# Four interleaved layers on one core: which head group VectorE takes, 163 adding transfers, epsilon on GpSimd

## The chip, the cores and the metric

One core of a Trainium2 chip runs the whole program in one launch. TensorE (PE) multiplies, VectorE (DVE), ScalarE (ACT) and GpSimd (POOL) work on tiles of 128 partitions, and SyncE (SP) and GpSimd start the DMA transfers. PSUM has eight banks of 128 x 512 float32 values here. The metric is the device time of one execution in microseconds (us), lower is better. The time of the kernel before is the median of three executions.

## The reference

The input x has 2048 rows of 512 values. Four layers are added to it in turn: A, B, A, B, with the same weights for both A and both B.

```python
def _A_ref(x, wq, wk, wv, wo):          # 32 query heads of 16, one key and value head
    q = (x @ wq).reshape(B, S, H, Dh).transpose(0, 2, 1, 3)
    k = x @ wk
    v = x @ wv
    scores = einsum("bhqd,bkd->bhqk", q, k) * (Dh ** -0.5)
    p = softmax(scores, axis=-1)
    o = einsum("bhqk,bkd->bhqd", p, v)
    return o.transpose(0, 2, 1, 3).reshape(B, S, H * Dh) @ wo
def _B_ref(x, wqkv, wo):                # linear attention, 32 heads of 16
    pq, pk = phi(q), phi(k)             # phi(t) = where(t > 0, t + 1, exp(t)) + 1e-6
    kv = einsum("bhsd,bhse->bhde", pk, v)
    z = einsum("bhsd->bhd", pk)
    o = einsum("bhqd,bhde->bhqe", pq, kv) / (einsum("bhqd,bhd->bhq", pq, z) + 1e-6)
    return o.transpose(0, 2, 1, 3).reshape(B, S, D) @ wo
x = x + A(layernorm(x)); x = x + B(layernorm(x)); x = x + A(layernorm(x)); x = x + B(layernorm(x))
```

The layer norm adds 1e-5 (epsilon) to the variance and has no weights.

## The kernel before

**The plan.** The kernel has no fixed loops over instructions. A planner (class Planner) runs a small simulation while the program is being built: every operation has an assumed duration, an assumed latency after it, a priority and the operations it depends on. When an engine of the simulation is free, the ready operation of the lowest priority number is put next on that engine. The order that comes out is written into the program; on the chip each engine follows its own order and waits on semaphores. A wrong duration in the plan doesn't make a wrong result, it makes an engine wait behind an operation whose input isn't there yet. Transfers have a cost of their own in the plan: a queue time `dmaq` is pushed forward by the first number of `xfer`, and the transfer lands the second number after that.

**Layer A (run_a, L = 0 and 2).** Queries are cut into 16 tiles of 128 rows, keys into 16 tiles of 128, and the 32 heads into two halves (par) of four groups j = 0..3 with four heads each. A block is one key tile with one head group: a score matmul writes 128 keys x (4 heads x 128 queries) into one PSUM bank (line 958). There are 64 blocks for each query tile and half, 2048 a layer. They are held in segments (class Seg): `left` lists the blocks not yet taken, `need[j]` counts the value matmuls that group j will take. Four value matmuls, one for each group, run side by side on TensorE, each in 32 of its columns (line 1012); a segment is done when each group has had its `need[j]`, and a round that lacks a group leaves that quarter of the array idle.

**Two ways to the exponential.** ScalarE takes groups of two or three blocks in one instruction (line 1134, function act_stream) and leaves bfloat16 probabilities in a PT buffer. VectorE takes single blocks (functions alone, dve_open, dve_split, dve_take): one add and maximum writes an int16 whose bits, read as bfloat16, are a rough exponential (line 1215). To make it exact enough, three shifted copies of it are needed, so that four value matmuls with four weighted copies of V stand for one. A block on VectorE thus raises `need[j]` by three. The copies are made for four blocks (a chunk, 128 x 2048) at a time: an add of a constant on VectorE (line 1263, dve_shifts), or, for at most one of the three copies of a chunk, an **adding transfer** (line 1292, dma_shift). For that, SyncE first fills a free FB buffer with the constant (the filling transfer, line 1283, prime) from a row `shift_row` (cst) in device memory, and GpSimd then starts a DMA that adds the chunk onto it. FB buffers are the working store of VectorE's way: 12 of their own, and others lent from tiles that rest (xn, wq, wo2, sacc, OBB), which is why the profile shows the same step under several tile names.

**Who takes which block.** ScalarE's groups never hold the same head group twice; Seg.take(js) gives the first block of the group with the most blocks left that isn't in js. VectorE takes from the back of a segment some way ahead of ScalarE (dve_pick: over `CHT` blocks ahead, `ENDL` at the end), by the same rule. VectorE starts when all keys of the layer are there (KGATE).

**Numbers that steer it.** BLO, BLS, BLT and DXB bound VectorE's backlog at which it is given another block; FBO, FBS and FBP are counts of free FB buffers kept back; DQ bounds the backlog of `dmaq` at which an adding transfer is still taken; PGEN, DPF, DXF and DTAIL are the plan's times of a transfer (starting it, filling, adding, landing); DMIN stops the transfers before the last segments. TUNE[0] is set at layer 0 and stays; TUNE[2] is put over it at layer 2.

**Layer norm (ln_tile, line 801).** For each of 16 tiles and four layers: statistics on VectorE (lines 810, 811), variance plus epsilon into ve on VectorE (line 812), the power -0.5 into rs on GpSimd (line 814), then the normalised tile xn on VectorE (line 817), which is transposed for the projections.

**Layer B (run_b)** lies mostly beside the attention of its neighbours.

**The start.** GpSimd fills FB buffer 11 with the constant (line 691) and SyncE writes one row of it to device memory as shift_row (line 692), with low priority, among the constants of the start.

Of the kernel before, what the change touches and what calls it, by code (L numbers as in the profile page):

```python
# [7 lines left out]
FP32 = mybir.dt.float32  # L8
I16 = mybir.dt.int16
ACTF = mybir.ActivationFunctionType  # L10
ALU = mybir.AluOpType

PE, AC, DV, PO, SP = "pe", "act", "dve", "pool", "sp"
ENGS = (PE, AC, DV, PO, SP)

P = 128
S, D, H, DH = 2048, 512, 32, 16
T = S // P
# [325 lines left out]
class Seg:  # L344
# [11 lines left out]
    def take(self, js, back=False):  # L356
        n = [sum(1 for b in self.left if b[1] == j) for j in range(4)]
        js = [j for j in range(4) if j not in js and n[j]]
        if not js:
            return None if back else self.left.pop(0)  # L360
        j = max(js, key=lambda j: n[j])
        mine = [b for b in self.left if b[1] == j]
        b = mine[-1] if back else mine[0]
        self.left.remove(b)
        return b
# [13 lines left out]
LAG = 0.15  # L379
# [16 lines left out]
BLS = 1.4  # L396
BLO = 5.0
DXB = 2.0
BLT = 2.5
# [11 lines left out]
ENDL = 12  # L411
NSH = 4
# [6 lines left out]
FBO = 2  # L419
FBS = 4  # L420
AHEAD = 20
CHT = 19
PSH = False
STICK = 1.5
# [3 lines left out]
DSH = 1  # L428
DMIN = 4
NPRE = 2  # L430
PGEN = 1.1
DPF = 2.5
DXF = 4.5
DTAIL = 2.5
DQ = 4.0
FBP = 6
TUNE = {0: {"FBS": 5, "AHEAD": 15, "LAG": 0.15, "ENDL": 12, "FBO": 0, "BLO": 7.0, "DXB": 1.6, "BLT": 3.2},
        2: {"FBS": 3, "DXB": 1.6, "ENDL": 9, "BLS": 1.0}}


def bass_interleave_layers__grouped_kv_mqa__linear_attn_block__prompt_kernel(
# [12 lines left out]
    op = pl.op  # L454
    sb = nc.alloc_sbuf_tensor
# [18 lines left out]
    xn = sb("xn", [P, NXN, D], BF16)  # L474
    st = sb("st", [P, T, 2, 6], FP32)
    mv = sb("mv", [P, T, 2], FP32)
    ve = sb("ve", [P, T], FP32)
    rs = sb("rs", [P, T], FP32)
    mhalf = sb("mhalf", [P, 1], FP32)
    ident = sb("ident", [P, P], BF16)  # L480
    mask8 = sb("mask8", [P, 8, 17], BF16)
# [11 lines left out]
    NFB = 12  # L493
    FB = sb("FB", [P, NFB, CHB * 512], BF16)
# [179 lines left out]
    def pool_op(fn, writes, reads=(), dur=0.2, prio=0.0):  # L674
        return op({PO: (dur, fn)}, reads=reads, writes=writes, prio=prio)
# [10 lines left out]
    cst = nc.dram_tensor("shift_row", (1, CHB * 512), I16, kind="Internal").ap()  # L686

    def fb_keys(i):
        return [("FB", i, h) for h in range(CHB)]

    pool_op(lambda e: e.memset(FB[:, NFB - 1, :].bitcast(I16), DSH * 128 // NSH), fb_keys(NFB - 1), dur=1.2, prio=8.0)
    op({SP: (0.54, lambda e: e.dma_start(cst, FB[0:1, NFB - 1, :].bitcast(I16)))}, reads=fb_keys(NFB - 1), writes=["cst"], prio=8.0, lat=2.5, dma=True)
    pool_op(lambda e: e.memset(kmask[:, 1:2], KSC), ["kmask"], dur=0.1)
    for j in range(4):
        for r, v in ((0, KSC), (1, 0.0)):
# [42 lines left out]
    def until(*keys):  # L738
        for k in keys:
            yield ("ops", pl.ws(k))  # L740
# [60 lines left out]
    def ln_tile(L, t, prio, far=False, crit=False):  # L801
        c = ring(L, t)
        hk = host(L, ("xnT", c)) if c >= 4 else ()
        cols = slice(c * P, (c + 1) * P)
        if t in two:
            two.discard(t)
            n = 2
        else:
            n = 1
            op({DV: (0.6, lambda e: e.bn_stats(st[:, t, 0, :], x_sb[:, t, :]))}, reads=[("x", t)], writes=[("st", t)], prio=prio, lat=0.13)  # L810
        op({DV: (0.09, lambda e: e.bn_aggr(mv[:, t, :], st[:, t, 0:n, :]))}, reads=[("st", t)], writes=[("mv", t)], prio=prio, lat=0.13)
        op({DV: (0.07, lambda e: e.tensor_scalar(out=ve[:, t:t + 1], in0=mv[:, t, 1:2], scalar1=1e-5, scalar2=None, op0=ALU.add))},  # L812
           reads=[("mv", t)], writes=[("ve", t)], prio=prio, lat=0.16)
        op({PO: (0.55, lambda e: e.tensor_tensor(out=rs[:, t:t + 1], in0=ve[:, t:t + 1], in1=mhalf[:], op=ALU.pow))},  # L814
           reads=[("ve", t), "mhalf"], writes=[("rs", t)], prio=prio - 9.0)
        i = yield ("acq", xn_pool, prio)
        op({DV: (0.325, lambda e: e.tensor_scalar(out=xn[:, i, :], in0=x_sb[:, t, :], scalar1=mv[:, t, 0:1], scalar2=rs[:, t:t + 1],
                                                op0=ALU.subtract, op1=ALU.mult))},
           reads=[("x", t), ("mv", t), ("rs", t)], writes=[("xn", i)], prio=prio, port=True, behind=host(L, ("xn", i)) if i >= 2 else ())
        if far:  # L820
            o = dmat(xnT[:, :, cols], xn[:, i, :], [("xn", i)], [("xnT", c)], prio, hk)
            pl.give_after(xn_pool, i, [o])
            return
        yield from until(("xn", i))
        if crit:
            bs = yield from acq2(prio)
            o = tr2(xn[:, i, :], [("xn", i)], bs, prio)
            pl.give_after(xn_pool, i, [o])
            halves(bs, lambda h: xnT[:, 2 * h:2 * h + 2, cols], ("xnT", c), prio, lambda b, h: bank_bf(b)[:, 0:2, :], hk)
            return  # L830
        b = yield ("acq", banks, prio)
# [117 lines left out]
    def run_a(L):  # L949
# [114 lines left out]
        def act_stream():  # L1064
# [11 lines left out]
            while True:  # L1076
# [3 lines left out]
                while len(group) < size[s_] and split is None and state["si"] < len(segs):  # L1080
                    sg = segs[state["si"]]
                    if not sg.left:
                        state["si"] += 1
                        if state["si"] == len(segs) - BACK:
                            recall([("FB", NFB + 4), ("FB", NFB + 5)])
                        continue
                    if len(group) == GA - 1 and size[s_] == GA:
                        split = dve_split({g_[2] for g_ in group})
                        if split is not None:
                            continue  # L1090
                    js = {g_[2] for g_ in group}
                    blk = sg.take(js)
                    while any(("K", L, kt) not in pl.flags for kt in (sg.kts if L else blk[:1])) or ("Q", L, sg.t) not in pl.flags:
                        if group:
                            break
                        yield ("flag", next((("K", L, kt) for kt in (sg.kts if L else blk[:1]) if ("K", L, kt) not in pl.flags), ("Q", L, sg.t)))
                    else:
                        group.append((sg,) + blk)
                        continue
                    sg.left.insert(0, blk)  # L1100
                    break
# [4 lines left out]
                n = len(group)  # L1106
# [64 lines left out]
        def dve_pick(js):  # L1171
            si = state["si"]
            ahead = 0
            for k in range(si, si + 5):
                if k >= len(segs):
                    continue
                sg = segs[k]
                ahead += len(sg.left)
                if ahead <= (CHT if si < len(segs) - 1 else ENDL):
                    continue  # L1180
                if len(sg.left) > sg.blocks * (1.0 - DMAX) and all(("K", L, kt) in pl.flags for kt in sg.kts) and ("Q", L, sg.t) in pl.flags:
                    b_ = sg.take(js | {x[2] for x in chunk["blk"] if x[0] is sg}, back=True) or sg.take(js, back=True)
                    if b_ is not None:
                        return (sg,) + b_
            return None
# [88 lines left out]

        def prime():
            yield ("flag", ("K", L, T - 1))
            yield from until("cst")
            while state["si"] < len(segs) - DMIN:
                if len(primed) >= NPRE or len(fb_pool.free) <= FBP or fb_pool.wait:
                    yield ("sleep", 0.2)  # L1280
                    continue
                g_ = yield ("acq", fb_pool, 9.0)
                o = op({SP: (0.54, lambda e, g_=g_: e.dma_start(fbs[g_].bitcast(I16), cst.to_broadcast([P, CHB * 512])))}, reads=["cst"], writes=fb_keys(g_), prio=9.0,
                       lat=0.2, dma=True, behind=guest(L, "FB", g_), xfer=(DPF, DTAIL))
                primed.append((g_, o))
            while primed:
                g_, o = primed.pop()
                pl.give_after(fb_pool, g_, [o])
# [607 lines left out]
```

## Time and profile before

| | |
|---|---|
| median of three executions | 1501.57 us (1501.36 to 1502.54) |
| the profiled execution, its own time | 1502.7 us |
| its span, first to last instruction | 1501.0 us |
| granted TensorE clock, mean | 1.0 |
| instructions | 36621 |

The page gives for each engine its busy time, its share of the span and its instructions. The view of groups lists instructions by line, engine and operation: the tile written <- the tiles read, the shape, the count, then busy time and mean duration, then the idle time of the engine just before them with what released it. Durations of neighbouring instructions overlap, so the distance between two starts on the timeline is the better price of one more instruction. The view by windows gives the busy time and the count (x) of each engine in a stretch of the span, then the clock, the share of the 16 DMA engines and GB/s.

### The profile page before, as it was taken

The page shows a single profiled execution, that of the slowest core. Times are in us where ns is not written, and L with a number is a line of the kernel's source. Part 1 is how long each engine was busy: PE and PEld are TensorE (multiplying, and loading weights), DVE is VectorE, ACT ScalarE, POOL GpSimd, SP SyncE. Part 2 cuts the span into 40 slices and gives each one's busy share as a digit, 9 for nine tenths or more (in the row PEclk, how much of TensorE's full clock was granted, in tenths as well). Part 3 has the DMA queues.
Part 4 walks back from the last instruction along what each step waited for, and adds up shares of the span by engine and source line. Part 5 has one row for each costly group of instructions (what it writes and reads, how often), then busy time and mean ns, then how long its engine had stood idle before and what let it go on. Part 6 is the DMA issues. An engine that isn't in the chain of part 4 may idle for free.

```text
span 1501.0 us, 36621 instructions
## 1 busy us (share of the span) xinstructions
PE 1418.2 (94%) x14634; PEld 514.3 (34%) x14745; DVE 1426.3 (95%) x2684; ACT 1453.6 (97%) x1519; POOL 167.2 (11%) x230
## 2 busy tenths in 40 slices
PE   7999999999999999999999999999999999999998
PEld 4433333332232233323744332333332332323335
DVE  8899999999999999998867799999999999999997
ACT  7999999999999999999799999999999999999996
POOL 5100101101010100000111101111111111100001
PEclk9999999999999999999999999999999999999999
DMA  4624533433443434001000124446464674552001
GB/s 107 176 65 114 124 65 92 106 89 78 104 104 66 92 93 89 30 15 58 2 2 1 30 51 106 111 120 152 116 152 111 151 157 108 134 131 58 16 2 57
DMA packets 71738, 128.76 MB, mean 86 GB/s; under 512 B 37521, under 2 KB 44177, under 8 KB 71570
## 3 DMA queue, kind: packets, MB, share of 16 engines
q0 software_dynamic: 14832, 54.01, 19.2%
q1 hardware_dynamic: 56738, 72.41, 16.4%
q8 instruction: 119, 1.95, 0.5%
q14 instruction: 49, 0.40, 0.1%
HBM read 62.42 MB, written 2.10 MB: 43 GB/s over the span
## 4 chain that ended last, share of the span: by engine, by line
PE 35%; DVE 33%; ACT 24%; issue 7%; POOL 0%; ACTq 0%; POOLq 0%
ACT PT L1134 16%; PE ps L1012 13%; DVE FB L1215 12%; PE ps L958 11%; DVE FB L1263 8%; PE ps L730 4%; ACT xnT L1134 3%; ACT OBB L1134 3%; PE ps L891 2%; DVE OBB L1215 2%; PE ps L1057 2%; PE ps L1365 1%; DVE sacc L1215 1%; DVE xn L1215 1%; DVE wq L1263 1%
## 5 line engine op out<-in xcount | busy, mean ns | idle before, releaser
L1134 ACT ACTIVATE PT<-ps 128x1024 bf16<-128x1024 f32 (+1 forms) x951 | 1016.4, 1179 | 6.3 <-PE ps L1012 3.0
L958 PE MATMUL ps<-QT,KM 32*128 32x512 bf16 x4096 | 536.5, 385 | 43.0 <-ACT PT L1134 18.0
L1215 DVE TENSOR_SCALAR FB<-ps 128x512 int16<-128x512 f32 x790 | 521.0, 682 | 5.6 <-PE ps L958 4.4
L1012 PE MATMUL ps<-FB,VW 128*32 128x512 bf16 x3126 | 501.5, 385 | 9.5 <-ACT PT L1134 3.1
L1012 PE MATMUL ps<-PT,V 128*32 128x512 bf16 x2108 | 431.4, 386 | 2.2 <-ACT PT L1134 1.3
L958 PEld LDWEIGHTS ps<-QT,KM 32*128 32x128 bf16 x4096 | 134.1, 91 | 442.2 <-ACT PT L1134 216.2
L1134 ACT ACTIVATE xnT<-ps 128x1024 bf16<-128x1024 f32 (+1 forms) x241 | 267.8, 1158 | 3.7 <-PE ps L1012 2.0
L1263 DVE TENSOR_SCALAR FB<-FB 128x2048 int16<-128x2048 int16 (+1 forms) x354 | 237.2, 678 | 0.3
L1134 ACT ACTIVATE OBB<-ps 128x1024 bf16<-128x1024 f32 (+1 forms) x167 | 190.1, 1170 | 1.2 <-PE ps L958 0.5
L1012 PEld LDWEIGHTS ps<-FB,VW 128*32 128x32 bf16 x3126 | 123.3, 94 | 146.9 <-issue 86.0
L1012 PE MATMUL ps<-xnT,V 128*32 128x512 bf16 x530 | 144.5, 385 | 0.7 <-ACT xnT L1134 0.3
L1057 PE MATMUL ps<-QT,V 128*32 128x512 bf16 (+6 forms) x571 | 132.1, 316 | 0.8 <-DVE FB L1215 0.4
L1012 PEld LDWEIGHTS ps<-PT,V 128*32 128x32 bf16 x2108 | 104.8, 94 | 70.5 <-issue 44.4
L1012 PE MATMUL ps<-OBB,V 128*32 128x512 bf16 x372 | 108.9, 385 | 1.5 <-ACT PT L1134 0.5
L1292 POOL DMA_DIRECT2D FB<-FB x56 | 52.1, 930 | 422.0 <-DVE FB L1215 247.6
L814 POOL TENSOR_TENSOR rs<-ve,mhalf 128x1 f32<-128x1 f32 x64 | 46.0, 722 | 463.1 <-DVE ve L812 462.9
L1012 PE MATMUL ps<-xn,VW 128*32 128x512 bf16 x256 | 69.3, 384 | 0.1
L1012 PE MATMUL ps<-sacc,VW 128*32 128x512 bf16 x246 | 68.2, 384 | 0.7 <-ACT PT L1134 0.6
L730 PE MATMUL ps<-wqkv,xnT 128*128 128x512 bf16 (+1 forms) x209 | 65.5, 369 | 3.0 <-issue 1.7
L1057 PEld LDWEIGHTS ps<-QT,V 128*32 128x32 bf16 x571 | 44.4, 95 | 63.2 <-issue 43.3
L1012 PE MATMUL ps<-wq,VW 128*32 128x512 bf16 x244 | 64.2, 384 | 1.2 <-ACT PT L1134 1.1
L1012 PE MATMUL ps<-OBB,VW 128*32 128x512 bf16 x240 | 58.5, 385 | 3.2 <-ACT PT L1134 1.4
(206 smaller groups left out, 1662.2 us busy)
## 6 DMA issues: line engine op xcount, KB each, us to landing
FB<-shift_row SPq DMA_DIRECT2D x81, 512.0 KB, 4.6
FB<-FB POOLq DMA_DIRECT2D x56, 512.0 KB, 5.0
wo<-shift_row SPq DMA_DIRECT2D x10, 512.0 KB, 4.3
FB<-sacc POOLq DMA_DIRECT2D x8, 512.0 KB, 5.1
FB<-xn POOLq DMA_DIRECT2D x6, 512.0 KB, 5.4
wo<-FB POOLq DMA_DIRECT2D x6, 512.0 KB, 4.9
xn<-shift_row SPq DMA_DIRECT2D x6, 512.0 KB, 4.5
FB<-wo POOLq DMA_DIRECT2D x5, 512.0 KB, 4.9
```

What stands on the lines that cost most here:

```text
L730: return e.matmul(dst, lhsT=l, rhs=r, start=(k == 0), stop=(k == len(pairs) - 1))
L814: op({PO: (0.55, lambda e: e.tensor_tensor(out=rs[:, t:t + 1], in0=ve[:, t:t + 1], in1=mhalf[:], op=ALU.pow))}, reads=[("ve", t), "mhalf"] ...
L891: ins = e.matmul(dst[:, g * P:(g + 1) * P], lhsT=lhs(g, k), rhs=rhs(k), start=(k == 0), stop=(k == FT - 1))
L958: return e.matmul(bank(b), lhsT=KM[r, sg.par, kt * P:(kt + 1) * P], rhs=QT[r, sg.t, :], start=True, stop=True)
L1012: ins = e.matmul(ps[32 * j:32 * j + 32, ACC * 512:(ACC + 1) * 512], lhsT=V[:, kt, :] if w is None else VW[:, kt, w, :], rhs=ap, start=(k = ...
L1057: o = op({PE: (n / 2400.0, lambda e: e.matmul(ps[32 * j:32 * j + 32, b * 512:b * 512 + n], lhsT=V0[:], rhs=QT[:, sg.t, 0:n], start=st, sto ...
L1134: ex = op({AC: (0.051 + 0.4267 * n, lambda e, n=n, s_=s_, p_=p_: e.activation(pts[p_][:, 0:n * 512], ps[:, s_ * 512:(s_ + n) * 512], ACTF. ...
L1215: o = op({DV: (0.602, lambda e: e.tensor_scalar(out=dst.bitcast(I16), in0=bank(b), scalar1=VB, scalar2=VLO, op0=ALU.add, op1=ALU.max))}, w ...
L1263: o = op({en: (du, lambda e, w=w, g_=g_: e.tensor_scalar(out=fbs[g_][:, 0:n].bitcast(I16), in0=fbs[f_][:, 0:n].bitcast(I16), scalar1=float ...
L1292: o = op({PO: (PGEN, lambda e: e.dma_start(fbs[g_].bitcast(I16), fbs[f_].bitcast(I16), accum_op=ALU.add))}, reads=fb_keys(f_), writes=fb_k ...
L1365: o = op({PE: (0.12, lambda e, c=c: e.transpose(ps[:, b * 512 + c * P:b * 512 + (c + 1) * P], src[:, c * P:(c + 1) * P], identF[:]))}, rea ...
```

## The change

- **Choice of group.** With EVEN, VectorE takes from the back the group with the smallest `need`, not the one with the most blocks left. With AVOID, ScalarE's take leaves out the group of smallest `need` where it can. With CHE = 8, VectorE may go nearer to ScalarE than CHT blocks (though over 8), for groups that have the smallest `need` only.
- **Adding transfers.** Numbers that steer them are changed: fewer FB buffers are kept back before a filling transfer (FBP 6 to 4), the queue may be longer (DQ 4 to 6), the plan's times of a transfer are altered (as they come out: PGEN 1.1 to 0.95, DPF 2.2 for 2.5, DXF 4.5 as before, DTAIL 2.0 for 2.5). The plan holds 163 adding transfers.
- **Other numbers.** The backlog bounds (BLO 7 to 3.5, BLS 1.4 to 2.3 and 1.0 to 1.7, BLT 3.2 to 2.8, DXB 1.6 to 2.0), CHT 19 to 26, FBS 5 to 3 in layer 0, AHEAD 15 to 8, FBO 0 to 1, LAG, STICK, and DMIN 4 to 3 in layer 2.
- **Epsilon.** The add of line 812 goes from VectorE to GpSimd, ahead of the power on the same engine.
- **shift_row.** The fill of the constant goes from GpSimd at the start to VectorE when layer 0 has its keys, one partition high, and the write of the row follows it there.

```diff
@@ Seg.take
-        j = max(js, key=lambda j: n[j])
+        j = min(js, key=lambda j: (self.need[j], -n[j])) if back and EVEN else max(js, key=lambda j: n[j])
@@ numbers
-PGEN = 1.1
-DPF = 2.5
-DXF = 4.5
-DTAIL = 2.5
+EVEN = True
+CHE = 8
+AVOID = True
+PGEN = 0.95
+DPF = 2.2
+DXF = 2.8
+DTAIL = 1.6
 DQ = 4.0
-FBP = 6
-TUNE = {0: {"FBS": 5, "AHEAD": 15, "LAG": 0.15, "ENDL": 12, "FBO": 0, "BLO": 7.0, "DXB": 1.6, "BLT": 3.2},
-        2: {"FBS": 3, "DXB": 1.6, "ENDL": 9, "BLS": 1.0}}
+FBP = 4
+TUNE = {0: {"DXF": 4.5, "DTAIL": 2.0, "CHT": 26, "FBO": 1, "FBS": 3, "AHEAD": 8, "BLS": 2.3, "BLT": 2.8, "FBP": 4, "DQ": 6.0, "DMIN": 4, "LAG": 0.25, "BLO": 3.5, "STICK": 2.5, "DXB": 2.0},
+        2: {"CHE": 8, "DMIN": 3, "NPRE": 2, "BLS": 1.7}}
@@ start
-    pool_op(lambda e: e.memset(FB[:, NFB - 1, :].bitcast(I16), DSH * 128 // NSH), fb_keys(NFB - 1), dur=1.2, prio=8.0)
-    op({SP: (0.54, lambda e: e.dma_start(cst, FB[0:1, NFB - 1, :].bitcast(I16)))}, reads=fb_keys(NFB - 1), writes=["cst"], prio=8.0, lat=2.5, dma=True)
@@ ln_tile
-        op({DV: (0.07, lambda e: e.tensor_scalar(out=ve[:, t:t + 1], in0=mv[:, t, 1:2], scalar1=1e-5, scalar2=None, op0=ALU.add))},
-           reads=[("mv", t)], writes=[("ve", t)], prio=prio, lat=0.16)
+        op({PO: (0.1, lambda e: e.tensor_scalar(out=ve[:, t:t + 1], in0=mv[:, t, 1:2], scalar1=1e-5, scalar2=None, op0=ALU.add))},
+           reads=[("mv", t)], writes=[("ve", t)], prio=prio - 9.0, lat=0.08)
@@ act_stream
-                    blk = sg.take(js)
+                    if AVOID and L >= 0 and max(sg.need) > min(sg.need) and len(sg.left) > 8:
+                        low = min(range(4), key=lambda j: sg.need[j])
+                        blk = sg.take(js | {low}) if len(js | {low}) < 4 and any(b_[1] not in js | {low} for b_ in sg.left) else sg.take(js)
+                    else:
+                        blk = sg.take(js)
@@ dve_pick
+                low = set()
                 if ahead <= (CHT if si < len(segs) - 1 else ENDL):
-                    continue
+                    if ahead <= CHE or max(sg.need) == min(sg.need):
+                        continue
+                    low = {j for j in range(4) if sg.need[j] > min(sg.need)}
+                    if len(low | js) == 4:
+                        continue
...
-                    b_ = sg.take(js | {x[2] for x in chunk["blk"] if x[0] is sg}, back=True) or sg.take(js, back=True)
+                    b_ = sg.take(js | low | {x[2] for x in chunk["blk"] if x[0] is sg}, back=True) or sg.take(js | low, back=True)
@@ prime
+            if L == 0:
+                row = FB[0:1, NFB - 1, :].bitcast(I16)
+                op({DV: (0.6, lambda e: e.memset(row, DSH * 128 // NSH))}, writes=fb_keys(NFB - 1), prio=1.0)
+                op({SP: (0.54, lambda e: e.dma_start(cst, row))}, reads=fb_keys(NFB - 1), writes=["cst"], prio=1.0, lat=2.5, dma=True)
```

More of the change, by code (lines that the diff above doesn't have):

```diff
@@ L476, in bass_interleave_layers__grouped_kv_mqa__linear_attn_block__prompt_kernel @@
     mv = sb("mv", [P, T, 2], FP32)
+    rs = sb("rs", [P, T], FP32)
     ve = sb("ve", [P, T], FP32)
-    rs = sb("rs", [P, T], FP32)
     mhalf = sb("mhalf", [P, 1], FP32)
```

## The prediction

> **What bounds the kernel now.** I read the page first: busy times, with shares of the span, and the chain of waits by engine.
>
> ```profile
> PE 1418.2 (94%) x14634; PEld 514.3 (34%) x14745; DVE 1426.3 (95%) x2684; ACT 1453.6 (97%) x1519; POOL 167.2 (11%) x230
> ...
> PE 35%; DVE 33%; ACT 24%; issue 7%; POOL 0%; ACTq 0%; POOLq 0%
> ```
>
> Three engines are at 94% or more and share the chain; an average can't name the bound. So next the view by windows, over the two attentions (60 to 700 is layer 0, 860 to 1440 layer 2); its columns are PE, PEld, DVE, ACT, POOL.
>
> ```profile
> 60.00:620.00 560.00, 531.19 (x5462) 175.45 (x5500) 558.04 (x1003) 555.82 (x561) 54.96 (x57) 1.00 0.39 90
> ...
> 860.00:1350.00 490.00, 466.12 (x4791) 150.38 (x4823) 486.25 (x879) 487.92 (x507) 61.12 (x65) 1.00 0.53 123
> ```
>
> VectorE is busy for 558.0 of 560 us and 486.3 of 490, ScalarE for 555.8 and 487.9: both are full. TensorE's 95% is softer, because it runs filler matmuls when it has nothing else, and its weight loads for scores mostly wait for ScalarE to give banks back. The group of fillers, and that wait:
>
> ```profile
> L1057 PE MATMUL ps<-QT,V 128*32 128x512 bf16 (+6 forms) x571 | 132.1, 316 | 0.8 <-DVE FB L1215 0.4
> ```
>
> ```profile
> PEld ps L958 <- ACT PT L1134: 216.2, 576, 1.0
> ```
>
> So the exponentials bound it, split over two full engines; what one is relieved of is worth something only if blocks move over from the other. The split, from the groups with shapes kept apart (128x1024 is two blocks, 128x1536 three):
>
> ```profile
> L1134 ACT ACTIVATE PT<-ps 128x1024 bf16<-128x1024 f32 x745 | 753.9, 1085 | 4.4 <-PE ps L958 2.2 <-PE ps L1012 1.4
> L1134 ACT ACTIVATE PT<-ps 128x1536 bf16<-128x1536 f32 x206 | 307.4, 1517 | 2.0 <-PE ps L1012 1.6 <-PE ps L958 0.2
> L1134 ACT ACTIVATE xnT<-ps 128x1024 bf16<-128x1024 f32 x193 | 200.7, 1075 | 3.6 <-PE ps L1012 2.0 <-PE ps L891 1.1 <-PE ps L958 0.3
> L1134 ACT ACTIVATE OBB<-ps 128x1024 bf16<-128x1024 f32 x129 | 135.6, 1069 | 1.0 <-PE ps L958 0.5
> L1134 ACT ACTIVATE xnT<-ps 128x1536 bf16<-128x1536 f32 x48 | 71.0, 1493 | 0.1
> L1134 ACT ACTIVATE OBB<-ps 128x1536 bf16<-128x1536 f32 x38 | 56.9, 1509 | 0.2 <-PE ps L1012 0.2
> ```
>
> ```profile
> sum 1501.00, ACT 1388.97; mean ACT 198.42
> ```
>
> The last row is the windows' sum for line 1134 alone, over the whole span. ScalarE takes 2 x (745 + 193 + 129) + 3 x (206 + 48 + 38) = 3010 blocks in 1389.0 us, 0.46 us each; the other 2 x 2048 - 3010 = 1086 are VectorE's, about 272 chunks. ScalarE's waits before these groups add up to 11.3 us.
>
> **The adding transfers.** 163 are planned after the change. How many are there now? Line 1292 alone in two stretches of the windows (POOL busy, count), then its largest group (minimum, median and longest start in ns), and that group's landing:
>
> ```profile
> 60.00:620.00 560.00, 44.09 (x44) 1.00 0.39 90
> ...
> 860.00:1350.00 490.00, 49.38 (x53) 1.00 0.53 123
> ```
>
> ```profile
> L1292 POOL DMA_DIRECT2D FB<-FB x56: 852/872/1367, 50.6 to 1357.4; - x56
> ```
>
> ```profile
> FB<-FB POOLq DMA_DIRECT2D x56, 512.0 KB, 5.0
> ```
>
> 44 and 53 in these two; the same view has two each in the stretches 0 to 60, 700 to 860 and 1350 to 1440, which makes 103. I read 163 as the total: 163 more would be 266, nearly every chunk, while the plan books a filling (2.2) and an adding transfer (4.5) one after the other, 6.7 us for each pair, or 157 pairs in these 1050 us. So 60 are added, and each takes one shift of 2048 off VectorE. What that is worth there, by the distance of starts:
>
> ```profile
> 1010.04 0.15 DVE L812 TENSOR_SCALAR ve<-mv 128x1 f32<-128x1 f32 x1
> 1010.11 0.68 DVE L1263 TENSOR_SCALAR FB<-FB 128x2048 int16<-128x2048 int16 x1
> 1010.71 0.68 DVE L1215 TENSOR_SCALAR OBB<-ps 128x512 int16<-128x512 f32 x1
> 1011.31 0.40 DVE L817 TENSOR_SCALAR xn<-x_sb,mv,rs 128x512 bf16<-128x512 bf16 x1
> ```
>
> A shift costs 0.60 us, a block's first pass 0.60, an epsilon 0.07. Relief 60 x 0.60 = 36.0 us, less 0.6 for the fill of shift_row that VectorE takes over (as a pass of the same width; its row's write adds one start on SyncE, and the first filling transfer waits for it to land): 35.4. A block moved to VectorE costs it 0.60 + three quarters of a shift for its share of a chunk, 0.45: 1.05, and relieves ScalarE of 0.46. Both stay full when 35.4 - 1.05 x = 0.46 x, so x = 23.4 blocks and the end comes 0.46 x 23.4 = **10.8 us** earlier. On GpSimd the 60 starts add 60 x 0.87 = 52 us to 167: nothing queues there but the layer norm's powers and the copies of V. On TensorE 23 blocks add 70 value matmuls; the chain has a row for such a run:
>
> ```profile
> 994.15 1.62 PE ps L1012 x28
> ```
>
> 0.058 us each, so 4 us in all, under the 132 us of fillers. If that cover were gone, it would cost these 4.
>
> **Choice of group.** Its prize is in rounds of four value matmuls, 0.23 us each by that row. A block on VectorE adds three to one group; if groups now end one such block apart in each of the 64 segments, evening saves 64 x 3 x 0.23 = 44 us of TensorE. Bounds: nothing, since fillers stand where the saving would be, and ScalarE's whole wait of 11.3 us. TensorE is not first to be full, so I stay near the low end: **3 us**. The narrower choice could also leave VectorE without a block: it idled 5.7 us in the two long windows, so a few us either way; the backlog bounds are put here too, at nothing, from -5 to +5.
>
> **Epsilon on GpSimd.** VectorE saves 64 x 0.07 = 4.5 us. The add's duration on GpSimd is not in the trace; below lies a fill of one column, above it the power of one column on the same tiles:
>
> ```profile
> 2.18 0.09 POOL L706 MEMSET wts<- 128x1 f32 x1
> ```
>
> ```profile
> L814 POOL TENSOR_TENSOR rs<-ve,mhalf x64: 543/560/1156, 4.2 to 1468.8; 128x1 f32<-128x1 f32 x64
> ```
>
> 0.09 to 0.56; I take 0.2, nearer the fill as no power is taken. Per tile the add of 0.15 us leaves VectorE, so at the four places where a layer norm heads the chain (start, two handovers to B, one to A) it costs about 0.1 each, 0.4 in all, with 0 to 1.6 as bounds. Elsewhere the attention hides it. What it holds up on VectorE is taken to cancel the 4.5: the shifts alone, passes from SBUF to SBUF, are a third of VectorE's 1426 us, by the windows' sum for line 1263,
>
> ```profile
> sum 1501.00, DVE 473.00; mean DVE 67.57
> ```
>
> and 64 x 0.2 / 3 = 4.3. Why it should hold anything up is seen at the start:
>
> ```profile
> 4.77 2.18 DVE L817 TENSOR_SCALAR xn<-x_sb,mv,rs 128x512 bf16<-128x512 bf16 x1 [0.68 <-POOL rs L814]
> ...
> 5.01 1.80 POOL L691 MEMSET FB<- 128x2048 int16 x1
> ```
>
> The first normalised tile took 2.18 us where its like took 0.40, under a GpSimd fill of 1.80. The Trainium skill, SBUF — State Buffer, section Who interferes with whom, says that such a VectorE pass and a GpSimd instruction exclude each other on a shared pair of ports for a whole instruction; these rows agree.
>
> **The start.** That fill is the one that leaves. The tile gets back up to 1.78 us; the query weights' landing and the other constants may take some of it. I take **1.4**, bounds 0 to 1.8, and 1.0 net of the 0.4 above.
>
> **The sum.** 1501.0 - 10.8 - 3 - 1.0 = 1486.2 span. The profiled execution took 1502.7, 1.7 more than its span, and lay 1.1 above the median; so 1486.2 + 1.7 - 1.1 = **1486.8**, some 1487. Its own range is 1479 to 1497, by the bounds of the four terms (the choice -11 to +5, epsilon at 0.56 some 7 more on VectorE, a third of which, 0.46 / 1.51, reaches the end).
>
> **Rivals.**
>
> *TensorE is in the chain after all.* It has 35% of it, more than ScalarE. If evening really frees 44 us and the chain takes its 35%, that is 15 us in place of 3: 1475. Against it: the fillers, and scores that wait 216 us for ScalarE.
>
> *The adding transfers land late (slower).* What ended the waits of the value matmuls and their weight loads, all of it, by the view of line 1012 (us, times); no transfer is among it.
>
> ```profile
>   issue: 176.3, 780
>   ACT PT L1134: 41.6, 108
>   DVE sacc L1345: 11.8, 30
>   ACT xnT L1134: 11.8, 30
>   ACT OBB L1134: 7.8, 23
>   DVE FB L1263: 7.6, 27
>   DVE FB L1215: 5.0, 22
>   DVE sacc L1348: 4.4, 13
>   DVE OBB L1215: 1.1, 4
> ```
>
> Before, an add was planned to land 1.1 + 0.3 + 4.5 + 2.5 = 8.4 us after its start; it took 5.0 in the median. Now the plan says 0.95 + 0.3 + 4.5 + 2.0 = 7.75, and the load grows: 53 pairs made a DMA share of 0.53 over 490 us, 4.9 us of all engines a pair, so 163 over 1050 us ask for 0.76. If queues stretch the landing by over 2.75 us, the value matmul of that copy stands at the head of TensorE's order, the next scores behind it, and ScalarE, with two sets of banks, starves. 14.8 us / 163 = 0.09 us of such waiting for each add on average is the point from which it is no gain; at 0.25 the time is 1487 + 41 = 1528, at 0.15 it is **1511**, which I take. For it: the margin shrinks while the share rises. Against it: the plan's own queue spaces pairs 6.7 us apart, above the 4.9 they use. The Trainium skill, SBUF — State Buffer, section on the bandwidth-pool intuition, has a transfer started by GpSimd slowed from 0.62 to 3.1 us while VectorE held the ports; the starts here took 0.87 in the median and 1.37 at most in the largest group beside a full VectorE, so the trace bears little of it out.
>
> *The relief is not used.* The lower backlog bounds (BLO 3.5 for 7, BLT 2.8 for 3.2) keep VectorE at 1086 blocks: it idles, ScalarE keeps its 1389 us, only the start's 1.0 remains: 1500.6.
>
> *The port eats the relief.* If each epsilon held VectorE for 0.56 us, 64 x 0.56 = 36 us less 4.5 leave 35.4 - 31.5 = 4 us of relief, worth 1.2: with the 3 and 1.0, 1496. The skill's rule named above is what would make every one of them block; VectorE passes that read PSUM, most of its time, speak against.
>
> **How the numbers follow.** Forecast 0.52; TensorE 0.18; late transfers 0.18; relief unused 0.07; port 0.05. A measurement of this kernel tells 0.2% (3 us) from no change. Faster: the forecast, the TensorE case and 0.03 of the port's, 0.73. Within 0.2%: 0.05 of the unused relief and 0.02 of the port's, 0.07. Slower: 0.18 and 0.02 of the unused relief, 0.20. The range from 1472 to 1504 takes in all but the late case and a part of TensorE's, some 0.8.
>
> **What would show it.** Right: 163 rows of line 1292; about 1110 blocks on line 1215, 2986 on ScalarE; 3 x 1110 / 4 - 163 = 670 VectorE shifts on line 1263, against 3 x 1086 / 4 - 103 = 712 now; both engines still over 99% busy in the attentions; no DMA among what line 1012 waits for; the first line 817 near 0.4 us. More fillers, with ScalarE's load as it is, would mean rounds were saved where nothing needed them. Wrong: VectorE with idle time and ScalarE at 3010 blocks (relief unused); value matmuls or scores released by an adding transfer, with ScalarE idle behind them (late); line 817 or 1263 longer than 0.68 us next to the epsilons (port).

## The result, and the profile after

The changed kernel takes 1508.05 us in the median of 19 executions (1501.68 to 1514.70), the kernel before beside it 1502.39 (1501.03 to 1505.67): a ratio of 1.0033, with a 95% interval of 1.0019 to 1.0046. It is a third of a per cent slower, and its executions spread over 13 us where those before spread over 5. Its own clock record goes with that: the execution at 1501.68 has a mean granted TensorE clock of 0.995, the one at 1514.70 has 0.984.

The change moved the line numbers: scores stand on line 959 (958 before), value matmuls on 1013 (1012), ScalarE's exponentials on 1139 (1134), VectorE's on 1225 (1215), its shifts on 1273 (1263), adding transfers on 1306 (1292), DMA transposes on 737 (736), epsilon, power and normalised tile on 813, 815 and 818. The page's busy times, and its chain, of the profiled execution (1501.68 us, span 1499.9):

```profile
PE 1403.9 (94%) x14791; PEld 509.3 (34%) x14906; DVE 1416.7 (94%) x2615; ACT 1444.2 (96%) x1511; POOL 245.8 (16%) x353
...
PE 20%; ACT 15%; DVE 13%; issue 5%; DMA 3%; POOL 1%; ACTq 0%; POOLq 0%
```

ScalarE's busy time fell by 9.4 us and VectorE's by 9.6; DMA, absent before, now has 3% in the chain. ScalarE's groups, by shape:

```profile
L1139 ACT ACTIVATE PT<-ps 128x1024 bf16<-128x1024 f32 x741 | 744.9, 1076 | 11.7 <-PE ps L959 10.3 <-PE ps L1013 0.4
L1139 ACT ACTIVATE PT<-ps 128x1536 bf16<-128x1536 f32 x205 | 303.5, 1505 | 1.2 <-PE ps L959 1.1
L1139 ACT ACTIVATE xnT<-ps 128x1024 bf16<-128x1024 f32 x190 | 194.8, 1068 | 6.5 <-PE ps L959 6.2
L1139 ACT ACTIVATE OBB<-ps 128x1024 bf16<-128x1024 f32 x137 | 141.0, 1068 | 0.2 <-PE ps L959 0.2
L1139 ACT ACTIVATE xnT<-ps 128x1536 bf16<-128x1536 f32 x48 | 69.7, 1485 | 0.7 <-PE ps L959 0.7
L1139 ACT ACTIVATE OBB<-ps 128x1536 bf16<-128x1536 f32 x29 | 43.6, 1502 | 3.0 <-PE ps L959 3.0
```

2 x (741 + 190 + 137) + 3 x (205 + 48 + 29) = 2982 blocks for ScalarE, so 1114 for VectorE: 28 have moved over, a few more than the 23 of the sum. But ScalarE now waits 23.3 us before these groups, 11.3 before, and almost all of it for scores. The windows of the two attentions (PE, PEld, DVE, ACT, POOL, then clock, DMA share, GB/s):

```profile
60.00:620.00 560.00, 527.75 (x5501) 170.23 (x5541) 548.39 (x972) 550.56 (x564) 96.06 (x107) 0.99 0.68 158
860.00:1350.00 490.00, 459.49 (x4859) 154.26 (x4895) 479.75 (x864) 480.13 (x494) 84.64 (x94) 0.99 0.69 159
```

Both engines that were full have idle time: VectorE 21.9 us here (5.7 before), ScalarE 19.3 (6.3 before). The work went down and the span didn't. Where TensorE waited for a transfer, the largest rows of the view of waits (total us, times, longest us; one stop can show twice, at a weight load, PEld, and at a matmul, PE):

```profile
PEld ps L1013 <- DMA FB<-FB: 7.3, 5, 4.1
...
PE ps L959 <- DMA OT<-Osb: 5.8, 2, 3.2
PEld ps L731 <- DMA OT<-Osb: 5.8, 2, 3.0
PE ps L1013 <- DMA FB<-FB: 5.5, 4, 3.6
...
PE ps L731 <- DMA OT<-Osb: 2.2, 1, 2.2
```

Two kinds of transfer hold TensorE up: adding transfers (FB<-FB) and the DMA transposes of the attention's output (OT<-Osb, line 737, started by SyncE for the projection of 12 query tiles in each layer A). Landing times of all adding transfers, then of the transposes (minimum, median, longest; 60 were started, the trace has the landing of 57 after the change and of 59 before), first after the change and then before it:

```profile
DMA to landing us min/median/max: 4.4/5.5/11.4
```

```profile
DMA to landing us min/median/max: 2.4/2.7/8.9
```

```profile
DMA to landing us min/median/max: 4.5/5.0/10.7
```

```profile
DMA to landing us min/median/max: 2.4/2.5/5.7
```

The medians hardly moved; the ends of the transposes did. The plan books 4 us for a transpose, whatever else is under way, and 7.75 us for an adding transfer that finds its queue empty, more behind others.

### The profile page after: what moved, and what is told of

It reads as the page before. It is cut to its first block, busy times and chain, and to the rows that moved or that the text cites. A ratio compares the mean times of both kernels' runs of the same rounds, so it can differ in the third digit from the quotient of the medians.

```text
span 1499.9 us, 37236 instructions
## 1 busy us (share of the span) xinstructions
PE 1403.9 (94%) x14791; PEld 509.3 (34%) x14906; DVE 1416.7 (94%) x2615; ACT 1444.2 (96%) x1511; POOL 245.8 (16%) x353
## 3 DMA queue, kind: packets, MB, share of 16 engines
q1 hardware_dynamic: 65378, 103.87, 23.3%
## 4 chain that ended last, share of the span: by engine, by line
PE 20%; ACT 15%; DVE 13%; issue 5%; DMA 3%; POOL 1%; ACTq 0%; POOLq 0%
ACT PT L1139 9%; PE ps L1013 6%; PE ps L959 6%; ACT xnT L1139 4%; DVE FB L1225 4%; PE ps L731 3%; DVE FB L1273 3%; PE ps L1058 2%; PE ps L892 1%; DMA FB<-FB 1%; DVE OBB L1225 1%; DVE sacc L1225 1%; DMA OBB<-FB 1%; DMA xn<-FB 1%; ACT phE L1467 1%
## 5 line engine op out<-in xcount | busy, mean ns | idle before, releaser
L1139 ACT ACTIVATE PT<-ps 128x1024 bf16<-128x1024 f32 (+1 forms) x946 | 1005.8, 1169 | 12.9 <-PE ps L959 11.4
L1225 DVE TENSOR_SCALAR FB<-ps 128x512 int16<-128x512 f32 x828 | 545.7, 683 | 18.2 <-PE ps L959 16.8
L1013 PE MATMUL ps<-FB,VW 128*32 128x512 bf16 x3247 | 452.5, 385 | 7.3 <-DVE sacc L1359 1.7
L1013 PE MATMUL ps<-PT,V 128*32 128x512 bf16 x2097 | 380.9, 388 | 13.8 <-ACT PT L1139 5.5
L1273 DVE TENSOR_SCALAR FB<-FB 128x2048 int16<-128x2048 int16 x365 | 244.9, 681 | 0.2
L1058 PE MATMUL ps<-QT,V 128*32 128x512 bf16 (+6 forms) x623 | 150.3, 318 | 1.3 <-DVE FB L1225 0.7
L1306 POOL DMA_DIRECT2D FB<-FB x77 | 77.0, 1001 | 426.1 <-DVE FB L1225 314.3
L1013 PE MATMUL ps<-xnT,V 128*32 128x512 bf16 x524 | 121.2, 388 | 1.3 <-ACT xnT L1139 0.6
L1013 PE MATMUL ps<-OBB,V 128*32 128x512 bf16 x361 | 83.5, 390 | 2.7 <-ACT PT L1139 1.4
L813 POOL TENSOR_SCALAR ve<-mv 128x1 f32<-128x1 f32 x64 | 30.7, 482 | 316.2 <-DVE mv L812 314.7
L1225 DVE TENSOR_SCALAR xn<-ps 128x512 int16<-128x512 f32 x81 | 53.7, 683 | 1.2 <-PE ps L959 1.0
```

What stands on the lines that cost most here:

```text
L813: op({PO: (0.1, lambda e: e.tensor_scalar(out=ve[:, t:t + 1], in0=mv[:, t, 1:2], scalar1=1e-5, scalar2=None, op0=ALU.add))}, reads=[("mv", ...
L1013: ins = e.matmul(ps[32 * j:32 * j + 32, ACC * 512:(ACC + 1) * 512], lhsT=V[:, kt, :] if w is None else VW[:, kt, w, :], rhs=ap, start=(k = ...
L1058: o = op({PE: (n / 2400.0, lambda e: e.matmul(ps[32 * j:32 * j + 32, b * 512:b * 512 + n], lhsT=V0[:], rhs=QT[:, sg.t, 0:n], start=st, sto ...
L1139: ex = op({AC: (0.051 + 0.4267 * n, lambda e, n=n, s_=s_, p_=p_: e.activation(pts[p_][:, 0:n * 512], ps[:, s_ * 512:(s_ + n) * 512], ACTF. ...
L1225: o = op({DV: (0.602, lambda e: e.tensor_scalar(out=dst.bitcast(I16), in0=bank(b), scalar1=VB, scalar2=VLO, op0=ALU.add, op1=ALU.max))}, w ...
L1273: o = op({en: (du, lambda e, w=w, g_=g_: e.tensor_scalar(out=fbs[g_][:, 0:n].bitcast(I16), in0=fbs[f_][:, 0:n].bitcast(I16), scalar1=float ...
```

## The experiments

Two theories stood against each other. **Late**: transfers land after the time that the plan booked, TensorE stands at the head of its order, and its clock falls behind the stop. **Epsilon**: GpSimd's add costs each layer norm more than was thought. A third was that the choice of group itself costs something. The plan's own end, which the planner has when a program is built, serves as a rough measure of what was lost to things that the plan had wrong: the kernel before ended 2.4 us behind its plan (1500.0), the changed one 28 us behind its own (1479.9). Ratios are against the kernel before, run beside each group on the same chip, with 95% intervals.

**The changed kernel again (x1), no edit.**

> The changed kernel once more, as the measure for the three runs beside it. Late theory: adding transfers and the transposes behind them land later than planned in a few places, TensorE stands at the head of its order for some us each time and its granted clock falls behind it; then the executions spread as before (1501 to 1515 us), the slower ones with the lower mean clock. Rival, epsilon: GpSimd's add takes 0.56 us where the plan has 0.10, in every layer norm, and the loss is the same in each execution: a spread as narrow as the kernel's before (1501 to 1506).

1506.84 us (1502.57 to 1517.27), ratio 1.0028 (1.0014 to 1.0042). The spread is as wide as in the first measurement, the slowest execution has the lowest clock (0.985), the fastest the highest (0.995). One stop, in the chain of waits of its profile (start, us, what):

```profile
1009.04 11.39 DMA FB<-FB
1020.48 0.60 PE ps L1013 x4
1021.08 0.54 PE ps L959 x2
...
1024.16 0.32 PE ps L959 x3
```

and the windows around it:

```profile
1012.00:1016.00 4.00, 4.00 (x49) 1.26 (x37) 3.97 (x8) 4.00 (x6) 0.31 (x1) 1.00 1.00 197
1016.00:1020.00 4.00, 0.93 (x15) 0.20 (x11) 1.92 (x4) 1.74 (x2) 0.56 (x1) 1.00 1.05 275
1020.00:1024.00 4.00, 3.52 (x23) 0.67 (x23) 1.38 (x2) 1.73 (x2) 0.00 (x0) 0.57 0.47 95
1024.00:1028.00 4.00, 4.00 (x43) 1.40 (x39) 3.79 (x7) 3.79 (x6) 0.86 (x1) 1.00 0.62 120
```

This stop shows the mechanism. An adding transfer started at 1009.04 was booked for 7.75 us and took 11.39. Two things made it late. GpSimd took 2.43 us to start it, where the plan has 0.95; that is 1.5 of the 3.6 us. The rest came while the DMA engines were full (share 1.00 and 1.05): SyncE had started three filling transfers, of 512 KB each, within 2 us.

```profile
1009.04 2.43 POOL L1306 DMA_DIRECT2D FB<-FB  x1 [2.33 <-DVE FB L1225]
```

```profile
1009.94 0.32 SPq L1297 DMA_DIRECT2D sacc<-shift_row  x1
1010.80 0.32 SPq L1297 DMA_DIRECT2D OBB<-shift_row  x1
1011.89 0.32 SPq L1297 DMA_DIRECT2D FB<-shift_row  x1
```

TensorE has 0.93 us of work in four; after that it is busy, but at a clock of 0.57, a set of scores takes 0.54 us in place of 0.32, and ScalarE and VectorE get 1.73 and 1.38 us of work in these four as well. In the two middle windows ScalarE loses 4.5 us, for a transfer that was 3.6 us late; half of that falls into the window of the low clock, in which the last 0.5 us of the stop lie too. The Trainium skill, TensorE: Matmul & The Clock Gate, section HAM oscillation, has TensorE's clock halved by a wait for a DMA that spans its activity window of about 3.4 us; the window of 0.57 behind this stop, 3.55 us by TensorE's timeline, agrees, but shorter stops had the same behind them (last section).

Such lateness is rare: of the 163 adding transfers in this profile ten landed later than the plan had booked for them, five of these by more than 1 us, and twelve transposes took longer than the 4.1 us that the plan gives them from start to landing. Before the change it was two adds, both by more than 1 us, and nine transposes.

**Short adds (x2).** The same order and the same waits, a quarter of the bytes:

```diff
-  ... e.dma_start(fbs[g_].bitcast(I16), fbs[f_].bitcast(I16), accum_op=ALU.add) ...
+  ... e.dma_start(fbs[g_][:, 0:512].bitcast(I16), fbs[f_][:, 0:512].bitcast(I16), accum_op=ALU.add) ...
```

> Order and waits of the changed kernel, but each adding transfer moves only the first 512 of its 2048 columns, so the other three quarters of that copy stay unshifted: the output is another. Late theory: with the adds' service cut to a quarter (the DMA share from 0.68 to some 0.45) nothing lands after its planned time, no value matmul waits for a DMA, the clock stays 1.0, and the time is the plan's with the epsilon loss left: 1482 to 1490 us, narrow. Rival, epsilon: no more than 3 us faster than the changed kernel. Third, TensorE or the choice of group is to blame: unchanged.

1485.58 us (1484.94 to 1486.51), ratio 0.9882 (0.9868 to 0.9896). With the order untouched, 21 us and the spread are gone, and the clock is 0.999. One wait for an adding transfer is left, and none for a transpose over 0.3 us:

```profile
PEld ps L1013 <- DMA FB<-FB: 2.0, 1, 2.0
PE ps L1013 <- DMA FB<-FB: 1.5, 1, 1.5
```

The one left is the late add of x1, here too with a start of 2.44 us on GpSimd; the row of the chain:

```profile
994.61 9.31 DMA FB<-FB
```

With a quarter of the bytes it is still 1.6 us late: the slow start's part stays, the rest is gone. Shorter transfers didn't make the engines' own instructions faster: ScalarE's groups of two blocks took 1080 ns (1079 in x1), VectorE's first passes 680 (681). So the late theory holds, and the choice of group and epsilon, still in, are not what made the kernel slow.

**Epsilon as a fill (x3).**

```diff
-  ... e.tensor_scalar(out=ve[:, t:t + 1], in0=mv[:, t, 1:2], scalar1=1e-5, scalar2=None, op0=ALU.add) ...
+  ... e.memset(ve[:, t:t + 1], 1.0) ...
```

> Order and waits of the changed kernel, but GpSimd's epsilon add is a fill of the same column with 1.0 (0.1 us, as the plan has it): the normalisation then leaves the variance out and the output is another. Epsilon rival: the chain of each layer norm is 0.45 us shorter, VectorE's 10.8 us of waits for rs fall to about 3 as before, and the time falls by 8 us or more. Late theory: at most 5 us faster, and the spread of executions stays.

1505.39 us (1502.20 to 1515.95), ratio 1.0022 (1.0007 to 1.0037): no difference from x1 that can be told, and the same spread. The add's rows, after and in x3 (minimum, median, longest ns):

```profile
L813 POOL TENSOR_SCALAR ve<-mv x64: 206/223/1754, 4.0 to 1467.8; 128x1 f32<-128x1 f32 x64
```

```profile
L813 POOL MEMSET ve<- x64: 99/100/1186, 4.0 to 1474.2; 128x1 f32 x64
```

The median add takes 0.22 us, not the 0.56 that my expectations of x1 gave as its price; some run to over 1 us, as does the fill, so that the mean of the 64 is 0.48 (0.33 for the fill). What held the long ones was not tried. That costs VectorE waits (for rs 10.8 us in the changed kernel, 7.3 here, 3.1 before), but it is not the cause of the loss.

**107 adds (x4).** `DQ` back to 4, `DPF` 5.0.

> The changed kernel with two numbers of the plan set back so that it takes 107 adding transfers in place of 163 (queue bound 4 for 6, filling booked at 5.0 for 2.2), the choice of group and epsilon as changed. Late theory: spaced like this nothing is late, VectorE takes 1086 blocks as before the change, and the time is about what the kernel before took less what the even rounds give: 1492 to 1500 us, narrow, so faster than both. Rival, epsilon or the choice of group: 1504 or slower, since both are still in.

1507.08 us (1502.60 to 1512.26), ratio 1.0021 (1.0006 to 1.0037). The expectation failed. The waits for transfers are small in its profile (for OT 1.7 us at most), but the clock fell from about 32 us on, before the first adding transfer (65.0 us):

```profile
28.00:32.00 4.00, 3.22 (x40) 1.30 (x38) 3.84 (x12) 4.00 (x5) 1.79 (x5) 0.97 0.33 66
32.00:36.00 4.00, 4.00 (x32) 2.28 (x29) 1.59 (x5) 3.08 (x3) 0.95 (x3) 0.50 0.48 98
```

It stayed at 0.50 until about 54 us. The changed kernel has the same 3.22 us of TensorE in 28 to 32 and kept 1.00. That profile is of its slowest execution; what lowered the clock, and why the other executions too end 8 us or more behind the plan (1494.5), was not found.

**The choice of group alone (x5).** EVEN, AVOID and CHE put into the kernel before, nothing else.

> The kernel before with the choice of group alone (EVEN, AVOID, CHE); transfers' numbers, bounds, epsilon and the start are those before. It comes out with 131 adding transfers, booked to land 8.4 us after their start, and 1109 blocks on VectorE; the plan itself ends at 1492.4 us, that of the kernel before at 1500.0. Late theory: with the longer booking few are late, so the chip follows the plan as it did before (2.4 us behind it): 1493 to 1499 us, faster than both kernels. Rival, the choice of group costs time by itself (less work keeps TensorE's clock up): 1503 us or slower with a clock under 1.0 and no DMA waits.

1498.58 us (1495.27 to 1503.79), ratio 0.9967 (0.9950 to 0.9983): faster than both kernels. The choice of group is no loss by itself. It came with 28 more adding transfers, so the gain isn't the choice's alone.

**The transfers' numbers alone (x6).** PGEN 0.95, DPF 2.2, DTAIL 2.0, DQ 6, FBP 4, FBS 3 and, in layer 2, DMIN 3, in the kernel before.

> The kernel before with the transfers' numbers alone (PGEN, DPF, DTAIL, DQ, FBP, FBS, DMIN as changed): 153 adding transfers, uneven groups as before; the plan ends at 1504.3 us. Late theory: the denser transfers land late here too, DMA waits appear on TensorE, the clock falls under 0.997 and the time is 10 us or more over the plan: 1514 to 1525 us with a wide spread. Rival, lateness needs the new choice of group or epsilon: 1505 to 1509, narrow.

1512.32 us (1508.64 to 1517.03), ratio 1.0059 (1.0040 to 1.0079): 8 us behind its plan, less than I expected and more than the rival. The waits are there without the new choice of group (adding transfers 3.9 us on TensorE, OT 1.5), but its profile kept a clock of 1.0: its one stop of more than 1.5 us on TensorE's matmuls was 2.0 us long.

**Transposes booked at 8 us (x7).**

```diff
-DTL = 4.0
+DTL = 8.0
```

> The changed kernel with one number altered: the plan books 8 us for a DMA transpose in place of 4, adding transfers as changed (163); the plan ends at 1487.3 us. If the transposes that the transfers push back (x1: three waits for OT, 2 to 3 us each) are half of the late theory, their waits are gone and the time is nearer to its plan by about half of what the changed kernel loses (some 27 us behind its plan): 1495 to 1502. If the adding transfers alone are to blame: still 20 us or more behind the plan, 1507 or slower.

1492.21 us (1491.34 to 1494.58), ratio 0.9928 (0.9914 to 0.9942). One number, and the kernel is 0.7% faster than the one before, in place of slower. Transposes still land late by the old booking (7.1 us at the longest), but nothing waits for one, and only 4.9 us separate chip and plan. The order is a new one, so luck has a part in it; x9 and x11 look at that.

**No adding transfers (x8).** The filling loop never runs.

> The changed kernel without any filling or adding transfer: all three copies of each chunk are made on VectorE, which takes 1045 blocks; the plan ends at 1511.5 us. It costs the whole relief of 163 transfers. Late theory: nothing is late, clock 1.0, and the chip ends some 6 us behind the plan as with the short adds (epsilon): 1515 to 1520 us, narrow. So 163 transfers that land in time would be worth about 30 us against it. Rival, epsilon or the clock: spread and distance from the plan as large as in the changed kernel, 1530 or more.

1515.38 us (1514.31 to 1524.50), ratio 1.0090 (1.0068 to 1.0112). Against x2, 163 adds are worth 1515.4 - 1485.6, some 30 us, when they land in time; the changed kernel kept 1515.4 - 1506.8, some 9 of them. The 30 us come to 0.18 for each add, which is the price in the sum (10.8 us for 60).

**No wait for OT (x9).** Order and all other waits kept; the 24 projections behind a DMA transpose read a slice of `wo` instead.

```diff
+            far = t < FARO
+            gone = set(pl.ws(("OT", m))) if far else set()
+            lhs = [wo[:, g, 0:P] if far else OT[:, m, g, :] for g in range(4)]
...
+        o.deps -= gone
```

> Order and all other waits of the changed kernel, but the output projection of the 24 query tiles that are transposed by DMA multiplies a slice of wo in place of OT, so that it reads nothing that the transpose writes and doesn't wait for it (the transposes still run): the output is another. If the transposes carry the loss: x1 waited 7.4 us for OT in three places and 6.9 us for adding transfers in six, and a stop of 3 us costs as much again by the clock, so 1493 to 1498 us with a clock of 0.996 or more. If the adding transfers carry it: 1502 us or slower, clock 0.993. The short adds (x2, 1485.6) removed both.

1495.53 us (1493.78 to 1498.38), ratio 0.9958 (0.9946 to 0.9971). What is left:

```profile
PEld ps L1014 <- DMA FB<-FB: 8.3, 5, 4.2
PE ps L1014 <- DMA FB<-FB: 6.4, 5, 3.7
...
PE ps L960 <- DMA xnT<-xn: 2.0, 1, 2.0
```

From x1 (1.0028) to x9 is 0.70%, from x9 to x2 (0.9882) another 0.76%: about half of the loss is the output's transposes, the other half adding transfers and the transposes of xn.

**Adding transfers booked 2 us later (x10).** `DTAIL` 4.0, transposes at 4.

> The changed kernel with the adding transfers booked 2 us later (DTAIL 4.0 for 2.0, so 9.75 us after their start) and the transposes still at 4; the order comes out anew, 158 adds, and the plan ends at 1501.9 us. If the transposes carry the loss, DMA waits for OT or xnT remain on TensorE and the chip ends 12 us or more behind the plan (1514 or slower), with few waits for adds. If the adds carry it, it ends 4 to 8 us behind it: 1506 to 1510, narrow.

1506.02 us (1504.67 to 1509.24), ratio 1.0031 (1.0019 to 1.0042), 4.1 us behind its plan: the other outcome. In this order one wait for OT, of 1.5 us, is left. So a late transpose isn't a matter of its booking alone; it also depends on what the order puts beside it. The later booking cost its 22 us in the plan, with the other numbers left as they were.

**Transposes at 6 us (x11).** `DTL` 6.0.

> The changed kernel with a DMA transpose booked at 6 us (8 in x7, 4 as changed); 159 adds, plan 1492.4 us. Transposes landed in 7.1 us at most in x7, so a few are still late at 6: between 5 and 15 us behind the plan, 1497 to 1507, and a clock between x7's 0.998 and the changed kernel's 0.992. If x7 was a lucky order and not the booking: no order between the three, 20 us behind the plan.

1504.23 us (1501.33 to 1507.44), ratio 1.0016 (1.0006 to 1.0026): 11.8 behind its plan, between x7 and the changed kernel. No wait for OT; two adding transfers hold TensorE's matmuls for 2.3 and 1.9 us. So x7 owes part of its time to an order in which few adds were late.

**Everything booked (x12).** `DTL` 8, `DXF` 2.8 and `DTAIL` 5.0, epsilon back on VectorE, and the steering numbers chosen anew in the plan for these bookings.

```diff
-TUNE = {0: {"DXF": 4.5, "DTAIL": 2.0, "CHT": 26, "FBO": 1, "FBS": 3, "AHEAD": 8, "BLS": 2.3, "BLT": 2.8, "FBP": 4, "DQ": 6.0, ...},
-        2: {"CHE": 8, "DMIN": 3, "NPRE": 2, "BLS": 1.7}}
+TUNE = {0: {"DXF": 2.8, "DTAIL": 5.0, "CHT": 26, "FBO": 0, "FBS": 2, "AHEAD": 4, "BLS": 1.0, "BLT": 3.6, "FBP": 4, "DQ": 4.0, "DMIN": 5, "LAG": 0.25, "BLO": 5.0, "STICK": 2.5, "DXB": 2.0, "CHE": 12, "ENDL": 12, "NPRE": 2},
+        2: {"CHE": 4, "DMIN": 3, "NPRE": 2, "BLS": 1.4, "DQ": 4.0, "LAG": 0.25, "ENDL": 9, "FBO": 0, "BLT": 2.8, "AHEAD": 20, "DXB": 2.0, "STICK": 2.5, "FBS": 4, "FBP": 3, "CHT": 22, "BLO": 3.5}}
```

> The changed kernel with a DMA transpose booked at 8 us, an adding transfer at 9 (DXF 2.8, DTAIL 5.0), epsilon back on VectorE, and the steering numbers chosen anew for these bookings by trying many sets in the plan: 187 adds, 1121 blocks on VectorE, plan 1477.3 us. Late theory: nothing of weight is late, the chip ends 3 to 7 us behind the plan: 1480 to 1486 us, faster than both kernels and than x7, narrow, clock 0.998 or more. Rival, at 187 adds the queues are too full for any booking: DMA waits again, 1490 or slower.

1483.57 us (1481.35 to 1488.07), ratio 0.9883 (0.9866 to 0.9901), with 187 adding transfers. Its windows, and all that TensorE waited for from adding transfers:

```profile
60.00:620.00 560.00, 536.55 (x5598) 174.40 (x5635) 557.11 (x999) 558.84 (x572) 94.31 (x99) 1.00 0.72 167
860.00:1350.00 490.00, 468.07 (x4991) 155.43 (x5026) 488.66 (x890) 486.96 (x515) 98.18 (x105) 1.00 0.88 206
```

```profile
PEld ps L1013 <- DMA FB<-wo: 1.2, 1, 1.2
PE ps L1013 <- DMA FB<-wo: 0.9, 1, 0.9
```

The DMA engines are fuller than in the changed kernel (0.88 against 0.69), transfers still land late (adding transfers 10.7 us at the longest, transposes 6.8), and yet both engines are full again: nothing needs them before they land.

## Why the prediction was wrong, point by point

- **The bound** was right: where both engines that share the exponentials are 99% busy in the attentions, in x2 and x12, the kernel is 1.2% faster than the one before.
- **Relief and blocks** were right: 163 adds; 1114 and 2982 blocks against the 1110 and 2986 forecast. So the relief was used. x2, where little is late, takes 1485.6 us, 17.5 less than the kernel before beside it; the sum said 14.8 less. The fill of shift_row took VectorE 1.77 us, where the sum has 0.6.
- **Choice of group**, 3 us, stays unmeasured by itself; x5 shows that it isn't a loss. At the sum's price its 28 more adds are worth 5.0 us, and it gained 4.9, so by this estimate little is left for the choice. Fillers went from 132 to 150 us, which would fit rounds saved where nothing needed them, but isn't shown to come from that.
- **Epsilon** at 0.2 us was right for the median (0.22), not for the mean (0.48). VectorE's waits for rs rose by 7.7 us; x3 can't tell what of it reaches the end. The port left no mark: VectorE's shifts within FB took 0.684 us in the mean, 0.680 before, its normalised tiles 0.41, 0.44 before.
- **The start** was worth more than the 1.0 net: the first normalised tile took 0.45 us in place of 2.18, and ScalarE's first exponential began 2.1 us earlier. How much of this reaches the end isn't shown. The rows of it, after and before:

```profile
10.55 1.94 ACT L1139 ACTIVATE PT<-ps 128x1024 bf16<-128x1024 f32 x2 [0.48 <-PE ps L959]
```

```profile
12.69 1.94 ACT L1134 ACTIVATE PT<-ps 128x1024 bf16<-128x1024 f32 x2 [0.70 <-PE ps L958]
```

- **The rival that came true** is the late landing, at 0.18. Its place was right: x1's add overran its 7.75 us by 3.6 and TensorE stood still for 3.55. That its price, 1511, is near the 1508 measured is luck: it put 0.15 us of waiting on each add, while TensorE waited 7.0 us for the 163 adds of x1, 0.04 each; transposes and the clock made up the rest. The step that failed is the one against it, "the plan's own queue spaces pairs 6.7 us apart, above the 4.9 they use". It reasons from means, while a stop comes from the longest few: an add took 10.7 us before the change already. And a spacing of bookings is not a spacing of starts: beside the late add of x1 three fillings were started within 2 us. Above all, it counts only the two kinds of transfer that the plan's queue knows. The transposes are in none of my terms: the plan gives each a fixed 4 us, they run on the same DMA engines, and of the 21 us that x2 shows to hang on the transfers, x9 puts about half on them. The row for it stood in the trace of before: a longest landing of 5.7 us against a booking of 4, with one wait of 0.7 us.
- What follows a stop was left out as well: in x1 TensorE's matmuls waited 16.3 us for transfers, 14.8 more than in x2, and the kernel took 21.3 us more than x2, so by this estimate the stops cost some 1.4 times their length. The clock behind them is part of it; how large a part isn't shown.

## What to carry to other kernels

Where the order is fixed beforehand, a transfer's booked time must be its late one, not its median, and every kind of transfer on the same DMA engines needs one, those of other steps too. Before adding traffic, look up the longest landing of each kind and set it beside what the order allows, and count a stop of TensorE at more than its length, for the clock behind it. When a kernel becomes slower though the bounding engines lost work, keep the order and shrink the suspected transfer: here that one run told the cause from the other parts of the change.

## What the runs showed of the hardware that I had not expected

- **The length of a stop doesn't decide the clock by itself.** At one place of the order, behind a late transpose, TensorE stood still for 2.45 us in x1 and for 2.67 in the changed kernel's profile. The windows of that place, first in x1, then in the changed kernel:

```profile
504.00:508.00 4.00, 3.03 (x40) 0.91 (x36) 4.00 (x7) 3.87 (x4) 0.00 (x0) 1.00 1.05 160
508.00:512.00 4.00, 2.52 (x12) 0.55 (x16) 1.00 (x3) 1.26 (x2) 0.00 (x0) 0.57 0.88 286
512.00:516.00 4.00, 4.00 (x31) 0.87 (x23) 2.94 (x5) 2.47 (x3) 0.00 (x0) 0.58 0.37 131
```

```profile
504.00:508.00 4.00, 2.00 (x24) 0.47 (x23) 3.04 (x6) 2.84 (x4) 0.00 (x0) 1.00 1.08 180
508.00:512.00 4.00, 3.33 (x34) 1.11 (x35) 2.89 (x5) 2.89 (x4) 0.00 (x0) 1.00 0.67 238
512.00:516.00 4.00, 3.46 (x39) 1.03 (x36) 3.95 (x8) 4.00 (x4) 0.00 (x0) 1.00 0.29 116
```

The shorter stop halved the clock, the longer one didn't. Behind a stop of 3.15 us at 420 in the changed kernel the windows had clocks of 0.71 and 0.50, and the clock fell 1.6 us after TensorE had stopped; in x1's stop of 3.55 us it fell after 3.6. In x4 it fell with no stop of that length ahead of it. Where it fell behind a stop in these two profiles, it stayed low for 3.4 or 6.8 us. What decides was not found, so no length of stop can be called safe from these runs.
- **Full DMA engines are no loss as such**: a share of 0.88 in x12 beside a full VectorE and ScalarE.
- **Starting an adding transfer can take GpSimd 2.43 us** where the median is 0.87. It happened to the late one of x1 and to its like in the changed kernel's profile, both of which landed after 11.4 us, and to the same one in x2.

```profile
1005.68 2.43 POOL L1306 DMA_DIRECT2D FB<-FB  x1 [2.29 <-DVE FB L1225]
```

Whether VectorE's passes held it up was not tried.
